# Issuing every second streamed weight piece from GpSimd's queue

## The chip, the cores and the metric

The kernel runs on one core of one Trainium2 chip. The metric is the device time of one execution in microseconds (us); lower is better. The engines are named as in the profile: PE (TensorE) with its weight loads PEld, DVE (VectorE), ACT (ScalarE), POOL (GpSimd) and SP (SyncE). A transfer (DMA) is issued by an instruction on the queue of SP or of POOL, and carried by 16 DMA engines that the queues share. In the profile, q1 (hardware_dynamic) holds the transfers that SP issued, q0 (software_dynamic) those of POOL.

## The reference: what is computed

Two independent attention layers on 2048 tokens of width 640, whose outputs stand side by side. Part A is a sliding, dilated local attention with 32 heads of 20. Part B, in which the change lies, is a recurrence over 64 segments of 32 tokens with 8 memory rows:

```
mem = mem0
for s in range(n_seg):                      # 64 segments
    h = concatenate([mem, x[32 s : 32 s + 32]])          # 40 x 640
    q, k, v = h @ Wq, h @ Wk, h @ Wv                     # 32 heads of 192: 6144 columns each
    p = softmax(mask(q k^T * scale))
    o = (p @ v) @ Wo                                     # 40 x 640
    mem = o[:8]; out[s] = o[8:]
```

The memory rows that a segment leaves are the input of the next one, so the segments follow each other. All of Wq, Wk, Wv and Wo is needed in each of them.

## The kernel before

Part A comes first, and during it part B's data are prepared: windows of x are gathered in DRAM, transposed and stored again (L353 to L380), part B's resident weights are loaded, and the weight pieces that don't fit on the chip are copied into DRAM tiles of their own, row by row as they will be wanted (`copy_streamed`, L297 to L308; tiles wcopy_k, wcopy_v, wcopy_o).

Part B cuts the weights into pieces ("units"). A k, q or v piece is 128 rows by 1536 columns (384 KB), an o piece 128 by 1280 (320 KB). `STREAMED` (L259, L260) lists those that are not resident. In each segment 24 are streamed: 11 of k, 2 of v, 11 of o; no q piece is. After the last segment, `project_late` (L656) goes through the o pieces four more times, so 11 o pieces are streamed four times more.

`get_unit` (L421 to L435) hands a piece to PE. A resident one is returned; a streamed one is loaded into a tile of the pool `wstream` (L404), which has `nbuf` = 6 slots, so that a load can begin when PE has read out the piece that stood in its slot. All of these loads are issued by SP, at L434. The users are `project32` (L475, matmuls at L483: 4 or, where 64 tokens are projected, 8 matmuls for each piece), `project_out` (L613, matmuls at L621) and `project_late` (L656, matmuls at L665).

A segment (L678 to L747) is written out by hand: projections of the four head groups, transposes, scores (L555), softmax (L560 to L572), probabilities (L580, transposed at L587), the mix with the values (L604), output projections (L621), and the memory rows for the next segment (L635). The order on PE and SP is the written one: the whole loop stands in

```python
with tc.manual_schedule(engines={mybir.EngineType.PE, mybir.EngineType.SP}):
    for s in range(n_seg):
        segment(s)
```

POOL, DVE and ACT are not in that set; the framework's planner orders their instructions when the program is built.

What POOL does in part B: it copies "late" tokens (the last 8 columns of a window, projected once in four segments and kept in tiles Lb) into QT and KT before the scores that read them (L528); it copies the same columns of the mixed output OT into OL (L611, 4 a segment); it clears a part of P (L578); and it issues three stores a segment, OL to DRAM (L728, 96 KB) and the two halves of the segment's output (L746, 15 KB each). In the last segment it also loads the stored OL back in pieces of 1.5 MB (`load_late`, L653, L654) for `project_late`. SP's other work in part B is one load of the segment's tokens HX (L467, 80 KB) and, in the first segment, resident pieces (L339).

`evacuate` (L461) copies PSUM to SBUF on ACT and DVE in turn; its line in the profile is L463.

Of the kernel before, what the change touches and what calls it, by code (L numbers as in the profile page):

```python
# [273 lines left out]
def part_b(ctx, tc, B_x, B_mem0, B_Wq, B_Wk, B_Wv, B_Wo, out, ident, n_seg, pre, nbuf, mid):  # L274
    nc = tc.nc
# [16 lines left out]
    def unit_cols(u):  # L292
        return 1280 if u[0] == "o" else 1536

    copied = {}
# [41 lines left out]
    def load_resident(units, engs):  # L337
        for k, u in enumerate(units):
            engs[k % len(engs)].dma_start(unit_tile(res[u], u), unit_src(u))  # L339
# [77 lines left out]
    wait.update(resident[n_pre + len(early):])  # L417

    ahead_of = []

    def get_unit(u):  # L421
        if u in res:
            if u in wait:
                wait.remove(u)
                load_resident([u], [nc.sync])
            return res[u]
        if wait:
            ahead_of.append(u)
            if len(ahead_of) > nbuf:
                v = next(v for v in resident if v in wait)  # L430
                wait.remove(v)
                load_resident([v], [nc.sync])
        t = wstream.tile([128, SLOT], BF16, tag="ws")
        nc.sync.dma_start(t[:, 0:unit_cols(u)], copied[u])  # L434
        return t[:, 0:unit_cols(u)]  # L435

    mask = cpool.tile([128, L], FP32)
# [37 lines left out]
    def project32(Xs, m, g, dcs=range(5), ps=None):  # L475

        if ps is None:
            ps = [ps_acc.tile([128, 384], FP32, tag="acc", name=f"acc{n}") for n in range(len(Xs))]
        for dc in dcs:
            w = get_unit((m, g, dc))  # L480
            for n, X in enumerate(Xs):
                for j in range(4):
                    nc.tensor.matmul(ps[n][32 * j:32 * j + 32, :], lhsT=X[:, dc, :],  # L483
                                     rhs=w[:, 384 * j:384 * j + 384],
                                     start=(dc == 0), stop=(dc == 4), tile_position=(0, 32 * j))
        return ps
# [126 lines left out]
    def project_out(Y, g, pairs=range(6)):  # L613
        for a in pairs:
            i = 6 * g + a
            w = get_unit(("o", i, 0))
            for r in range(2):
                c = 2 * a + r
                for gv in range(2):
                    n, at = 640 * r + 320 * gv, 64 * r + 32 * gv  # L620
                    nc.tensor.matmul(Y[at:at + 32, :], lhsT=OT[:, L * c:L * c + 32], rhs=w[:, n:n + 320],  # L621
                                     start=(i == 0), stop=(i == 23), tile_position=(0, at))
# [33 lines left out]
    def project_late(b):  # L656
        X = late_tokens(b).rearrange("p (t c) -> p t c", c=48)
        ps = [ps_acc.tile([128, 384], FP32, tag="acc", name=f"late{gv}") for gv in range(2)]
        for i in range(24):
            w = get_unit(("o", i, 0))  # L660
            for r in range(2):
                c = 2 * i + r
                for gv in range(2):
                    n = 640 * r + 320 * gv
                    nc.tensor.matmul(ps[gv][:, 0:320], lhsT=X[:, :, c], rhs=w[:, n:n + 320],  # L665
                                     start=(c == 0), stop=(c == 47))
        rows = out2.rearrange("(s n) d -> s n d", n=SEG)[LATE * b:LATE * b + LATE, SEG - M:SEG]
        for gv in range(2):
            if gv:
                y = one.tile([128, 384], BF16, tag="Vst", name="y")[:, 0:320]  # L670
            else:
                y = one.tile([128, 4, L], FP32, tag="t1", name="y")[:].rearrange("p a n -> p (a n)").bitcast(BF16)
            evacuate(y, ps[gv][:, 0:320])
            nc.gpsimd.dma_start(rows[:, :, Dm + 320 * gv:Dm + 320 * gv + 320], y)
# [83 lines left out]
def run_all(ctx, tc, A_x, A_wqkv, A_wo, B_x, B_mem0, B_Wq, B_Wk, B_Wv, B_Wo, out, ident):  # L758
    n_seg = B_x.shape[1] // 32

    def mid(emit_loads):
        with ExitStack() as actx:
            part_a(actx, tc, A_x, A_wqkv, A_wo, out, ident, emit_loads)

    part_b(ctx, tc, B_x, B_mem0, B_Wq, B_Wk, B_Wv, B_Wo, out, ident, n_seg=n_seg, pre=110000, nbuf=6,
           mid=mid)
# [59 lines left out]
```

## Time and profile before

| | us |
|---|---|
| three runs, median | 2056.71 |
| three runs, lowest and highest | 2046.49 to 2058.95 |
| the profiled execution | 2051.98 |
| its span, first to last instruction | 2050.0 |
| PE busy | 1856.2 |
| DVE busy | 1189.1 |
| ACT busy | 731.4 |
| POOL busy | 425.8 |

The page's first part has the busy time of each engine. Instructions that only issue a DMA are not counted as busy, so POOL's share does not hold its DMA issues. The third part splits the DMA traffic by queue: packets, MB, and the time its packets took as a share of what 16 engines have in the span. The chain is followed back from the last instruction to what released each step; its shares say where the span went. A group of instructions is shown as its line, engine and operation, with its busy time and the mean of one in ns, and, after the second bar, the idle time of the engine just before and what ended most of it. The DMA issues have the size of one and the median time from issue to landing.

### The profile page before, as it was taken

The numbers are of one execution on the slowest core, as the hardware profiler recorded it, in microseconds if no ns is written. First come the engines' busy times: TensorE is split into PE (matmuls) and PEld (weight loads), VectorE is DVE, ScalarE is ACT, GpSimd is POOL, SyncE is SP. The second block draws the span as 40 slices with busy tenths as digits, with TensorE's granted clock in tenths as the row PEclk, the third lists the DMA queues.
The fourth block names the chain that finished last, engine by engine and source line by source line (L and its number), as shares of the span: only waits on it lengthen the run. The fifth ranks groups of instructions, "written<-read, shape, count | busy, mean of one in ns | idle before, by whom it ended". The sixth has DMA issues, their size and how long they took to land.

```text
span 2050.0 us, 99035 instructions
## 1 busy us (share of the span) xinstructions
PE 1856.2 (91%) x42896; PEld 1136.2 (55%) x42896; DVE 1189.1 (58%) x3754; ACT 731.4 (36%) x2194; POOL 425.8 (21%) x1018
## 2 busy tenths in 40 slices
PE   7889999999899999999999898999999999999978
PEld 4555555555555555555555555555555555555557
DVE  5666565665566555566555566565556656665630
ACT  3454333333333333333333333333333333333310
POOL 2111212222221222221222221122222222222210
PEclk9999999999999999999999999999999999999989
DMA  8997999999999999999999999999999999999997
GB/s 252 311 321 260 338 332 317 337 329 325 318 324 323 313 341 322 308 329 324 321 335 323 319 320 313 328 331 330 327 327 325 335 320 340 331 328 324 327 321 232
DMA packets 302367, 654.89 MB, mean 319 GB/s; under 512 B 64297, under 2 KB 87401, under 8 KB 301929
## 3 DMA queue, kind: packets, MB, share of 16 engines
q1 hardware_dynamic: 289961, 624.64, 89.4%
q0 software_dynamic: 11968, 23.91, 3.3%
q8 instruction: 336, 5.51, 1.0%
q14 instruction: 102, 0.84, 0.1%
HBM read 623.77 MB, written 30.74 MB: 319 GB/s over the span
## 4 chain that ended last, share of the span: by engine, by line
PE 53%; DMA 30%; DVE 8%; issue 6%; SPq 2%; ACT 2%; POOL 0%; ACTq 0%; DVEq 0%; POOLq 0%
PE acc L483 25%; DMA t<-wcopy_k 19%; PE Y L621 8%; DMA t<-wcopy_o 8%; PE pt L496 5%; PE Sps L555 4%; PE OTps L604 3%; PE pq L95 3%; PE pt L587 2%; DMA t<-wcopy_v 2%; PE po L161 1%; SPq L378 1%; DVE sb L463 1%; DVE P L580 1%; PE py L172 1%
## 5 line engine op out<-in xcount | busy, mean ns | idle before, releaser
L483 PEld LDWEIGHTS <-HX 128*32 128x32 bf16 x19380 | 480.7, 97 | 345.3 <-issue 116.2
L483 PE MATMUL acc<-t,HX 128*32 128x384 bf16 x4200 | 293.4, 330 | 49.9 <-DMA t<-wcopy_k 44.4
L483 PE MATMUL acc<-wres_q,HX 128*32 128x384 bf16 x6460 | 330.9, 332 | 2.6 <-issue 2.1
L483 PE MATMUL acc<-wres_v,HX 128*32 128x384 bf16 x5812 | 320.6, 330 | 13.9 <-issue 13.8
L611 POOL COPY OL<-OT 128x96 bf16<-128x96 bf16 x256 | 172.6, 674 | 652.0 <-DVE OT L463 326.7
L463 DVE CAST sb<-acc 128x384 bf16<-128x384 f32 x308 | 170.9, 555 | 212.5 <-PE acc L483 184.6
L463 ACT CAST sb<-acc 128x384 bf16<-128x384 f32 x338 | 159.8, 473 | 320.4 <-PE acc L483 225.7
L621 PE MATMUL Y<-t,OT 128*32 128x320 bf16 x2816 | 195.1, 307 | 26.9 <-DMA t<-wcopy_o 21.6
L568 ACT ACTIVATE t<-t 128x160 f32<-128x160 f32 x256 | 86.2, 337 | 369.4 <-DVE t L567 368.6
L483 PE MATMUL acc<-wres_k,HX 128*32 128x384 bf16 x2908 | 211.1, 330 | 1.5 <-issue 1.0
L621 PE MATMUL Y<-wres_o,OT 128*32 128x320 bf16 x3328 | 207.6, 305 | 4.4 <-issue 4.4
L621 PEld LDWEIGHTS <-OT 128*32 128x32 bf16 x6144 | 136.1, 96 | 114.0 <-issue 42.3
L528 POOL COPY QT<-Lb 128x96 bf16<-128x96 bf16 x237 | 63.5, 268 | 604.0 <-PE Sps L555 552.5
L496 PE MATMUL pt<-ident,sb 128*128 128x128 bf16 x1938 | 173.0, 222 | 8.7 <-DVE sb L463 7.1
L463 DVE CAST OT<-OTps 128x120 bf16<-128x120 f32 x512 | 128.5, 275 | 67.0 <-PE OTps L604 62.6
L562 DVE SCALAR_TENSOR_TENSOR t<-Sps,mask 128x160 f32<-128x160 f32 x256 | 82.7, 323 | 133.0 <-PE Sps L555 127.2
L496 PEld LDWEIGHTS <-sb 128*128 128x128 bf16 x1938 | 110.4, 98 | 83.7 <-issue 29.6
L555 PEld LDWEIGHTS <-QT 128*64 128x64 bf16 (+1 forms) x4096 | 107.7, 109 | 86.1 <-issue 65.9
L463 ACT CAST OT<-OTps 128x120 bf16<-128x120 f32 x512 | 111.2, 259 | 107.1 <-PE OTps L604 98.1
L555 PE MATMUL Sps<-KT,QT 128*64 128x40 bf16 (+1 forms) x4096 | 141.5, 190 | 2.3 <-issue 2.2
L463 ACT CAST QT<-pt 128x384 bf16<-128x384 f32 (+1 forms) x177 | 84.9, 480 | 115.9 <-PE pt L496 115.9
L570 DVE TENSOR_REDUCE sm<-t 128x4 f32<-128x160 f32 x256 | 81.7, 319 | 76.5 <-ACT t L568 76.2
(89 smaller groups left out, 2283.7 us busy)
## 6 DMA issues: line engine op xcount, KB each, us to landing
t<-wcopy_k SPq DMA_DIRECT2D x704, 384.0 KB, 5.4
t<-wcopy_o SPq DMA_DIRECT2D x748, 320.0 KB, 4.9
t<-wcopy_v SPq DMA_DIRECT2D x128, 384.0 KB, 5.4
wres_q<-in_B_Wq_dram SPq DMA_DIRECT2D x20, 384.0 KB, 7.9
wres_v<-in_B_Wv_dram SPq DMA_DIRECT2D x18, 384.0 KB, 7.2
olate<-OL POOLq DMA_DIRECT2D x64, 96.0 KB, 5.7
ximages<-wres_v POOLq DMA_DIRECT2D x16, 320.0 KB, 6.1
HX<-ximages SPq DMA_DIRECT2D x64, 80.0 KB, 4.4
```

Source lines behind the costliest of these rows:

```text
L95: nc.tensor.matmul(pq[32 * d:32 * d + 32], lhsT=wcol[:, k, t, 4 * c + d, :], rhs=xTs[s][:, k, :], start=(k == 0), stop=(k == 4), tile_posi ...
L463: (nc.scalar.copy if copies["n"] % 2 else nc.vector.tensor_copy)(dst, src)
L483: nc.tensor.matmul(ps[n][32 * j:32 * j + 32, :], lhsT=X[:, dc, :], rhs=w[:, 384 * j:384 * j + 384], start=(dc == 0), stop=(dc == 4), tile_ ...
L496: nc.tensor.matmul(pt[:, c], lhsT=sb[:, 128 * c:128 * c + 128], rhs=ident, start=True, stop=True)
L528: nc.gpsimd.tensor_copy(tokens(T)[:, :, 32:L], b[:])
L555: nc.tensor.matmul(Sps[64 * g2:64 * g2 + 64, a, :], lhsT=QT[lo:hi, L * cc:L * cc + 64], rhs=KTt[lo:hi, cc, :], start=(g2 not in seen), sto ...
L562: nc.vector.scalar_tensor_tensor(out=t1[:], in0=Sps[:], scalar=scale, in1=mask[:].unsqueeze(1).to_broadcast([128, 4, L]), op0=ALU.mult, op ...
L568: nc.scalar.activation(t1[:], t1[:], ACTF.Exp)
L570: nc.vector.tensor_reduce(out=sm[:], in_=t1[:], axis=AX.X, op=ALU.add)
L604: nc.tensor.matmul(dst, lhsT=V[32 * a:32 * a + 32, e0:e1], rhs=PT[32 * a:32 * a + 32, late, half, :], start=(wide and late == 0 and half = ...
L611: nc.gpsimd.tensor_copy(OL[:, :, 12 * g:12 * g + 12].rearrange("p n c -> p c n"), tokens(OT)[:, :, 32:L])
L621: nc.tensor.matmul(Y[at:at + 32, :], lhsT=OT[:, L * c:L * c + 32], rhs=w[:, n:n + 320], start=(i == 0), stop=(i == 23), tile_position=(0, at))
```

## The change

A counter is kept of the streamed loads. The first, third, fifth and so on are issued by SP as before; the second, fourth and so on by POOL (`nc.gpsimd`). The tiles, the slots, the pieces, their sources and the order in which PE uses them stay. SP's order stays the written one, with every second load gone; the loads on POOL are placed among POOL's other instructions by the planner.

```diff
@@ -417,6 +417,7 @@
     wait.update(resident[n_pre + len(early):])
 
     ahead_of = []
+    streamed = [0]
 
     def get_unit(u):
         if u in res:
@@ -431,7 +432,8 @@
                 wait.remove(v)
                 load_resident([v], [nc.sync])
         t = wstream.tile([128, SLOT], BF16, tag="ws")
-        nc.sync.dma_start(t[:, 0:unit_cols(u)], copied[u])
+        streamed[0] += 1
+        (nc.sync if streamed[0] % 2 else nc.gpsimd).dma_start(t[:, 0:unit_cols(u)], copied[u])
         return t[:, 0:unit_cols(u)]
 
     mask = cpool.tile([128, L], FP32)
```

## The prediction, made before the changed kernel was run

> **What bounds the kernel now.** I read the page from the top (busy shares, slices, chain), then the stretch that the change touches, then the waits of SP's queue, then the one stretch where POOL's queue carries much traffic.
>
> ```profile
> PE 1856.2 (91%) x42896; PEld 1136.2 (55%) x42896; DVE 1189.1 (58%) x3754; ACT 731.4 (36%) x2194; POOL 425.8 (21%) x1018
> ...
> q1 hardware_dynamic: 289961, 624.64, 89.4%
> q0 software_dynamic: 11968, 23.91, 3.3%
> ...
> PE 53%; DMA 30%; DVE 8%; issue 6%; SPq 2%; ACT 2%; POOL 0%; ACTq 0%; DVEq 0%; POOLq 0%
> ...
> L483 PE MATMUL acc<-t,HX 128*32 128x384 bf16 x4200 | 293.4, 330 | 49.9 <-DMA t<-wcopy_k 44.4
> L621 PE MATMUL Y<-t,OT 128*32 128x320 bf16 x2816 | 195.1, 307 | 26.9 <-DMA t<-wcopy_o 21.6
> t<-wcopy_k SPq DMA_DIRECT2D x704, 384.0 KB, 5.4
> t<-wcopy_o SPq DMA_DIRECT2D x748, 320.0 KB, 4.9
> t<-wcopy_v SPq DMA_DIRECT2D x128, 384.0 KB, 5.4
> olate<-OL POOLq DMA_DIRECT2D x64, 96.0 KB, 5.7
> HX<-ximages SPq DMA_DIRECT2D x64, 80.0 KB, 4.4
> ```
>
> The reader is to see two resources that are nearly full together: PE is busy 91% of the span and SP's queue alone takes 89.4% of the DMA engines' time. The chain alternates between them, PE 53% and DMA 30%; SP's queue has 2% and POOL none. PE's named waits for streamed pieces are 44.4 + 21.6 = 66 us. The steady stretch, and the end of the last segment beside it, from the busy times by stretch:
>
> ```profile
> 300.00:1900.00 1600.00, 1470.73 (x36450) 883.39 (x36451) 956.19 (x3259) 579.77 (x1820) 347.01 (x851) 0.99 0.94 325
> 1955.00:1975.00 20.00, 11.03 (x169) 5.25 (x169) 4.82 (x19) 2.97 (x8) 2.10 (x5) 0.70 1.03 358
> ```
>
> Columns: length, busy us of PE, weight loads, DVE, ACT, POOL, granted clock, DMA share, GB/s. In the steady 1600 us PE is busy 92%, at a granted clock of 0.99, and the DMA engines 94% at 325 GB/s. What SP's queue waits for:
>
> ```profile
> SPq L434 <- PE acc L483: 614.9, 561, 3.3
> SPq L434 <- PE Y L621: 458.1, 385, 3.7
> ```
>
> SP sits at L434 until PE frees one of the six slots, 1.1 us at a time (1073.0 / 946). The queue is never late by itself; it is held by slots. Last, the DMA view of 1955 to 1975 us, in which L654 reads 1.5 MB pieces through POOL's queue beside SP's stream:
>
> ```profile
> q0 software_dynamic: 921, 3.88, 56.7%
> q1 hardware_dynamic: 1309, 3.24, 45.6%
> ...
> t<-wcopy_o SPq DMA_DIRECT2D x5, 320.0 KB, 11.6
> ...
> t<-wcopy_k SPq DMA_DIRECT2D x2, 384.0 KB, 15.6
> ```
>
> Both queues are served at once; POOL's gets 54% of the bytes, and SP's pieces land after 11.6 and 15.6 us in place of 4.9 and 5.4.
>
> **The change, part by part.** A segment streams 24 pieces (11 k, 2 v, 11 o) and the tail 4 x 11, so 1580 in all, which the DMA issues confirm (704 + 748 + 128). 790 of them move to POOL, 12 a segment. The sum stands against the profiled execution's own 2052.0 us (span 2050.0), which is 4.7 us under the median of the runs.
>
> *Off SP's queue.* 790 issues at 0.32 to 0.36 us (the minimum and the median of L434's issues for k and o) and as many semaphore instructions of 17 ns: about 280 us. They lie beside the slot waits above, so I take 0. The end on the good side is half of the chain's 1% for L434, 10 us. Without the cover of the slot waits it would have been the 280.
>
> *Onto POOL's queue.* POOL's nearest rows are its store of 128 rows (L728, 0.55 us an issue) and of 24 rows (L746, 0.51). 790 x 0.55 = 435 us, plus 13 us of semaphores. By segment: 12 x 0.55 = 6.6 us beside 6.1 us of copies (POOL's busy time from 1000 to 1028 us), 13 of 28 us; POOL's idle time hides them. The cover that counts is the slack of the late-token copies (L528, 426 of them, 0.27 us), which PE needs for the next scores. In the timeline one ends at 1014.09 and the scores start at 1016.01; the next ends at 1017.19 and the scores start at 1021.17. One issue ahead of a copy costs 0.55 of a slack of 1.9 to 4.0 us: 0. If a quarter of the 237 QT copies had no slack it would be 59 x 0.55 = 32 us, the upper end.
>
> *The wait that comes with them.* Each POOL issue now waits for a slot, in POOL's own order; behind it stand the copies of L528, the copy of OT (L611, 0.64 to 0.78 us), the memset of P, and the stores of L728 and L746. PE's scores wait for L528, the evacuations of the next mix for L611. PE and SP keep the written order, POOL does not, so a planner places these issues and the trace of before cannot show where. Slots and late tokens are both freed by PE in PE's order, so an issue put ahead of a copy should mostly be free before it. The nearest row is SP's slot wait: 1.1 us mean, inside the slack; the longest is 3.7, 1.8 over a slack of 1.9. Ends: 0, and once a segment 64 x 1.8 = 115 us. I take 5, nearer to the mean. At the start, POOL also has part A's stores (L176, to 188.6 us) ahead of the first pieces, which SP issues from 152 us; PE needs them from 188.5. Two to three issues late: at most 6 us, within the same 5.
>
> *The transfers.* The bytes are the same. DMA time per MB from the page: q0 0.033 x 2050 x 16 / 23.91 = 45.3 us, q1 46.9. Half the streamed bytes are 286 MB, so 286 x -1.6 / 16 = -29 us if the engines bound throughout. From the window of 20 us: q0 46.8, q1 45.0, so +32 us. The ends are of opposite sign; the window's row is a load through POOL, but of short rows under heavy load, so I stay near the middle: -5. Landing through POOL (5.7 us for 96 KB, a store) beside SP's 4.4 for 80 KB gives at most 1.3 us more, which the landing of five pieces in line (5.4 us against 1.1 us a piece) covers.
>
> *The order of arrival.* Now one queue brings pieces in the order of need. With two, a piece on SP's and the next on POOL's share the engines, so the needed one lands later and its successor earlier. Upper end: each of PE's 107 named waits (74 + 33) grows by a whole piece, 0.36 MB / 325 GB/s = 1.1 us: 118 us. Lower end: half of those waits go because the successor is already there: -33. In a steady pair the later and the earlier arrival cancel, and SP's three slots still hold work for the engines; I take +8, nearer to zero.
>
> The sum: 0 + 0 + 5 - 5 + 8 = +8, so 2060 on the profile's scale and 2065 on the runs' median.
>
> The Trainium skill (DMA: Bandwidth & Descriptors, section "Issuing engines are not separate DMA queues") says that DMAs from all issuing engines share the same 16 DMA engines, so that spreading them saves only issue time. By it alone the sum would be 2057; the 358 GB/s of the window with both queues agrees only if 325 is a matter of demand, not of the queue. The same page ("Queues, rings and completion order") says that each DMA engine takes turns between queues packet by packet; the 56.7% to 45.6% of the window is in keeping with it. It is the mechanism of the first rival.
>
> **The rivals.** *Shared engines make the needed piece late (slower).* Place: PE's waits on the pieces that stay on SP. For it: landings of 11.6 and 15.6 us in the window, PE busy only 11.03 of 20 us there. Against it: POOL then had transfers of 1.5 MB; now it holds about three of 0.36. Price: the 107 waits grow by half a piece, 0.55 us, = 59 us: 2116. It decides once PE's waits on pieces exceed 66 by more than 20 us.
>
> *POOL's order holds PE (slower).* A slot wait stands ahead of a late-token copy. For it: POOL already waits 619.6 us at L528 for PE, so what is queued there is released late. Against it: the slack. Price: one wait of 1.8 us in half of the segments, 58 us: 2115.
>
> *Two queues fill the engines better (faster).* For it: 358 GB/s at share 1.03 against 325 at 0.94, and 45.3 against 46.9 us per MB. Against it: PE is 92% busy, and the window had far more in flight than six slots allow. Price: two thirds of PE's 66 us go: 2057 - 44 = 2013.
>
> That the change does nothing at all (transfers hidden anyway) is the forecast without its 8 us.
>
> **How the numbers follow.** Within 1% of 2056.7 (2036 to 2077, about what this kernel's runs can tell apart): the forecast, 0.35, own range 2040 to 2077. Late pieces 0.27 and POOL's order 0.12, both above 2077: slower 0.39. Fuller engines 0.26, below 2036. The range runs from 2005, just beyond the faster rival, to 2130, beyond both slower ones by 15 us; some 0.2 is left out, mostly where both slower ones come together.
>
> **What would show it.** POOL's issues: 790 more at L434, near 0.55 us. Right forecast: PE's waits on wcopy pieces between 55 and 90 us, DMA share 0.93 to 0.95, L528 copies not the releaser of PE's scores. First rival: landings of SP's pieces clearly longer than POOL's, PE's waits above 90. Second: PE or PEld at L555 waiting for POOL. Third: over 332 GB/s from 300 to 1900 us. I am wrong if POOL's issue of a loaded piece takes far over 0.55 us, or if the planner lets one queue take most of the slots.

## The result and the profile after

The changed kernel takes 2109.48 us (median of 4 runs, 2107.29 to 2115.85) against 2051.6 beside it: a ratio of 1.0287, 95% interval 1.0237 to 1.0336, so 58 us slower. The profiled execution has a span of 2108.2 us at a clock of 0.979 (before: 2050.0 at 0.981). Two lines were added ahead of the load, one of them right before it, so that L434, L483, L528, L555, L611 and L621 of before are now L436, L485, L530, L557, L613 and L623.

The page of the changed kernel: busy times, queues, chain, the groups of the streamed pieces, and the DMA issues.

```profile
PE 1854.8 (88%) x42896; PEld 1136.5 (54%) x42896; DVE 1191.6 (57%) x3754; ACT 734.6 (35%) x2194; POOL 828.4 (39%) x1808
...
q1 hardware_dynamic: 176201, 336.36, 49.4%
q0 software_dynamic: 75168, 312.19, 41.2%
...
DMA 43%; PE 37%; DVE 8%; issue 6%; ACT 2%; SPq 2%; POOL 1%; POOLq 0%; ACTq 0%; DVEq 0%
...
L436 POOL DMA_DIRECT2D t<-wcopy_k x384 | 207.0, 540 | 444.4 <-PE acc L485 351.7
L485 PE MATMUL acc<-t,HX 128*32 128x384 bf16 x4200 | 286.2, 329 | 79.3 <-DMA t<-wcopy_k 46.1
...
L623 PE MATMUL Y<-t,OT 128*32 128x320 bf16 x2816 | 191.3, 309 | 67.3 <-DMA t<-wcopy_o 64.2
...
L557 PE MATMUL Sps<-KT,QT 128*64 128x40 bf16 (+1 forms) x4096 | 141.0, 190 | 1.2 <-POOL QT L530 0.9
...
t<-wcopy_k POOLq DMA_DIRECT2D x384, 384.0 KB, 5.2
t<-wcopy_o SPq DMA_DIRECT2D x406, 320.0 KB, 5.1
t<-wcopy_k SPq DMA_DIRECT2D x320, 384.0 KB, 4.9
t<-wcopy_o POOLq DMA_DIRECT2D x342, 320.0 KB, 5.6
t<-wcopy_v SPq DMA_DIRECT2D x64, 384.0 KB, 5.4
t<-wcopy_v POOLq DMA_DIRECT2D x64, 384.0 KB, 6.3
```

PE does the same work (1854.8 us against 1856.2) in a longer span. The chain's DMA share grew from 30% to 43%, at PE's expense (53% to 37%). The idle time ahead of the streamed matmuls went from 49.9 and 26.9 us to 79.3 and 67.3. POOL's busy time went from 425.8 to 828.4 us, chiefly by its 790 issues at 0.54 us: unlike SP's, the issues of POOL are counted as busy on the page, and those of its stores were so before as well. (The section on the profile before says otherwise.) The scores wait 0.9 us in all, once, for POOL's late tokens: POOL's copies hold next to nobody. The view of L436 says who waited for its loads:

```profile
who waited for it (us, times):
  PE acc L485: 76.9, 107
  PE Y L623: 64.2, 72
```

The same two rows of L434 in the kernel before:

```profile
  PE acc L483: 46.4, 79
  PE Y L621: 21.6, 33
```

PE's waits for pieces doubled, by 73 us. The steady stretch of the changed kernel:

```profile
300.00:1900.00 1600.00, 1433.62 (x35631) 862.75 (x35620) 936.48 (x3186) 569.24 (x1776) 682.16 (x1505) 0.99 0.93 317
```

The DMA engines moved 317 GB/s at a share of 0.93 (before: 325 at 0.94), so they were not overrun; they were given work later. Which pieces come late shows when each load is paired, in the trace, with the end of PE's last matmul on the piece six places before it, in e6 five (whose slot it takes), with its landing, and with PE's first matmul on it. Means over all pieces that PE used from 300 to 1900 us, in us, with the runs of the next section; the last column is the ratio less 1, times 2051.6:

| kernel | slot free to issue | issue to landing | slot free to landing | landing to use | slower by |
|---|---|---|---|---|---|
| before | 0.20 | 5.18 | 5.38 | 1.20 | |
| changed, SP's pieces | 0.05 | 5.18 | 5.22 | 1.53 | |
| changed, POOL's pieces | 0.46 | 5.45 | 5.91 | 0.83 | |
| changed, all | 0.25 | 5.31 | 5.57 | 1.18 | 59 |
| all on POOL (e1) | 1.01 | 5.13 | 6.14 | 0.95 | 122 |
| every second on ACT (e2) | 0.09 | 5.51 | 5.60 | 1.03 | 26 |
| early pieces on POOL (e3) | 0.32 | 5.29 | 5.60 | 1.11 | 48 |
| late pieces on POOL (e4) | 0.33 | 5.25 | 5.58 | 1.30 | 90 |
| five slots (e6) | 0.15 | 4.79 | 4.95 | 0.93 | 145 |
| HX on POOL (e8) | 0.17 | 5.14 | 5.31 | 1.22 | -5 |
| SP alone, held back (e9) | 0.76 | 5.15 | 5.91 | 0.95 | 81 |
| both queues late (e10) | 0.49 | 5.38 | 5.87 | 0.97 | 89 |
| all on ACT (e11) | 2.99 | 4.41 | 7.40 | 0.78 | 419 |

It is POOL's pieces that come late: 41% of them were used within 0.25 us of their landing, against 9% of SP's and 19% before. Over the whole span, PE's idle time just ahead of such pieces went from 42 us (70 times) to 125 us (151 times) for the pieces that the change gives to POOL, and from 29 us (45 times) to 25 us (31 times) for those that stay on SP. The mean from landing to use hardly moved (1.20 to 1.18 us), because SP's pieces came earlier while POOL's came later: the mean lead does not show the loss, the late pieces do.

POOL issues 0.41 us later after a slot is free than SP does, and its pieces land 0.27 us later after the issue. Against the kernel before, POOL's pieces land 0.53 us later after their slot is free: about half of that is the later issue, and half (0.27) the longer way from issue to landing. A few lines of POOL's timeline in the changed kernel, with start, duration, instruction, and in brackets the idle time before it and what ended it:

```profile
1003.22 0.55 POOL L436 DMA_DIRECT2D t<-wcopy_v  x1 [1.23 <-PE acc L485]
1006.78 0.55 POOL L436 DMA_DIRECT2D t<-wcopy_k  x1 [3.01 <-PE acc L485]
1007.32 0.54 POOL L436 DMA_DIRECT2D t<-wcopy_o  x1
1007.85 0.28 POOL L530 COPY QT<-Lb 128x96 bf16<-128x96 bf16 x1
...
1026.28 0.64 POOL L613 COPY OL<-OT 128x96 bf16<-128x96 bf16 x1 [1.19 <-DVE OT L465]
1026.79 0.54 POOL L436 DMA_DIRECT2D t<-wcopy_k  x1
1027.32 0.55 POOL L730 DMA_DIRECT2D olate<-OL  x1
1027.86 0.54 POOL L436 DMA_DIRECT2D t<-wcopy_k  x1
1028.51 1.02 POOL L748 DMA_DIRECT2D out_dram<-Ysb  x2
```

Two things are to be seen. Mostly POOL stands idle at a piece until PE frees the slot (1.23 us, 3.01 us), and a piece that has nothing ahead of it is still issued 0.32 to 0.38 us after the slot is free (means over a piece's 56 or 57 segments, for eight of POOL's twelve pieces). At the end of a segment the pieces queue up behind the copy of L613 and the stores: k0_3, k1_0 and k1_3 are issued 0.66, 0.78 and 0.85 us after their slot is free. Of POOL's mean of 0.46 us, then, some 0.35 is there without anything ahead, and some 0.11 is POOL's other work.

### The profile page after: what moved, and what is told of

The parts are those of the page before. It is cut to its first block, busy times and chain, and to the rows that moved or that the text cites. A ratio compares the mean times of both kernels' runs of the same rounds, so it can differ in the third digit from the quotient of the medians.

```text
span 2108.2 us, 98914 instructions
## 1 busy us (share of the span) xinstructions
PE 1854.8 (88%) x42896; PEld 1136.5 (54%) x42896; DVE 1191.6 (57%) x3754; ACT 734.6 (35%) x2194; POOL 828.4 (39%) x1808
## 3 DMA queue, kind: packets, MB, share of 16 engines
q8 instruction: 336, 5.51, 1.0%
## 4 chain that ended last, share of the span: by engine, by line
DMA 43%; PE 37%; DVE 8%; issue 6%; ACT 2%; SPq 2%; POOL 1%; POOLq 0%; ACTq 0%; DVEq 0%
DMA t<-wcopy_o 17%; DMA t<-wcopy_k 16%; PE acc L485 15%; DMA t<-wcopy_v 9%; PE Y L623 6%; PE Sps L557 3%; PE pq L95 2%; PE OTps L606 2%; PE pt L498 2%; PE late L667 2%; PE pt L589 1%; PE po L161 1%; SPq L378 1%; DVE t L564 1%; DVE OT L465 1%
## 5 line engine op out<-in xcount | busy, mean ns | idle before, releaser
L485 PEld LDWEIGHTS <-HX 128*32 128x32 bf16 x19380 | 483.3, 96 | 360.1 <-issue 126.7
L436 POOL DMA_DIRECT2D t<-wcopy_k x384 | 207.0, 540 | 444.4 <-PE acc L485 351.7
L485 PE MATMUL acc<-t,HX 128*32 128x384 bf16 x4200 | 286.2, 329 | 79.3 <-DMA t<-wcopy_k 46.1
L485 PE MATMUL acc<-wres_q,HX 128*32 128x384 bf16 x6460 | 323.6, 328 | 1.3 <-issue 0.8
L485 PE MATMUL acc<-wres_v,HX 128*32 128x384 bf16 x5812 | 320.4, 332 | 2.6 <-issue 2.4
L436 POOL DMA_DIRECT2D t<-wcopy_o x342 | 183.9, 538 | 286.3 <-PE Y L623 133.6
L613 POOL COPY OL<-OT 128x96 bf16<-128x96 bf16 x256 | 172.7, 675 | 255.9 <-DVE sm L573 110.9
L623 PE MATMUL Y<-t,OT 128*32 128x320 bf16 x2816 | 191.3, 309 | 67.3 <-DMA t<-wcopy_o 64.2
L623 PEld LDWEIGHTS <-OT 128*32 128x32 bf16 x6144 | 136.6, 96 | 155.3 <-issue 85.8
L623 PE MATMUL Y<-wres_o,OT 128*32 128x320 bf16 x3328 | 208.3, 305 | 1.9 <-issue 1.9
L485 PE MATMUL acc<-wres_k,HX 128*32 128x384 bf16 x2908 | 208.9, 329 | 0.5 <-ACT sb L465 0.3
L557 PEld LDWEIGHTS <-QT 128*64 128x64 bf16 (+1 forms) x4096 | 107.0, 109 | 84.9 <-issue 65.5
L557 PE MATMUL Sps<-KT,QT 128*64 128x40 bf16 (+1 forms) x4096 | 141.0, 190 | 1.2 <-POOL QT L530 0.9
```

The costliest lines, as they stand in the source:

```text
L436: (nc.sync if streamed[0] % 2 else nc.gpsimd).dma_start(t[:, 0:unit_cols(u)], copied[u])
L557: nc.tensor.matmul(Sps[64 * g2:64 * g2 + 64, a, :], lhsT=QT[lo:hi, L * cc:L * cc + 64], rhs=KTt[lo:hi, cc, :], start=(g2 not in seen), sto ...
L613: nc.gpsimd.tensor_copy(OL[:, :, 12 * g:12 * g + 12].rearrange("p n c -> p c n"), tokens(OT)[:, :, 32:L])
```

## The experiments

Three theories stood at the start. A: a piece from POOL starts and lands later, and PE waits. B: two queues share the DMA engines, which changes the order of arrival. C: POOL's other work stands ahead of the pieces. All kernels below compute the whole result; the ratios are against the kernel before on the same chip.

**All pieces on POOL (e1).**

```diff
-        (nc.sync if streamed[0] % 2 else nc.gpsimd).dma_start(t[:, 0:unit_cols(u)], copied[u])
+        nc.gpsimd.dma_start(t[:, 0:unit_cols(u)], copied[u])
```

> All 1580 streamed pieces are issued by POOL, so there is one queue for them again, in the order of need. Theory A (a piece from POOL starts about 0.6 us later after its slot is free, and pieces with less slack than that make PE wait): all pieces are late instead of half, so about twice the 58 us of the change, 2165 us (2130 to 2200). Theory B (two queues share the DMA engines, and the arrival out of order is the cost): back near the kernel before, 2052 us, at most 2075. Theory C (the other work in POOL's order stands ahead of the pieces): twice the cost again, and POOL's issues late mainly behind the copies of OT and the stores.

Measured: 2171.66 us, ratio 1.0596 (1.0537 to 1.0656). With one queue again B expects no loss; the loss doubled, as A and C expected. A piece lands 5.13 us after its issue, as with SP alone (5.18), so a load through POOL was not slower on its way when all went there; it is issued 1.01 us after its slot is free. The steady stretch of this kernel:

```profile
300.00:1900.00 1600.00, 1404.17 (x33960) 833.50 (x33952) 893.94 (x3031) 538.73 (x1692) 979.31 (x2082) 0.98 0.89 303
```

The DMA share falls to 0.89: engines idle for want of issued pieces. Part of the 1.01 us is C, POOL's own work, and part the issues of the pieces ahead, 0.54 us each; this run does not tell them apart.

**Which pieces go through POOL (e3, e4).** In place of the counter, a set of 12 pieces says which go to POOL, chosen by how long ahead of its use a piece landed in the kernel before. In e3 the early ones go to POOL, in e4 the others. The edit of e3, against the kernel before:

```diff
+    on_pool = {("k", 0, 1), ("k", 0, 3), ("k", 1, 0), ("v", 0, 0), ("k", 2, 1), ("k", 2, 4), ("o", 0, 0), ("o", 2, 0), ("k", 3, 1), ("o", 6, 0), ("o", 12, 0), ("o", 18, 0)}
...
-        nc.sync.dma_start(t[:, 0:unit_cols(u)], copied[u])
+        (nc.gpsimd if u in on_pool else nc.sync).dma_start(t[:, 0:unit_cols(u)], copied[u])
```

> 12 pieces a segment go through POOL as in the change, but those that landed 1.25 us or more ahead of their use in the kernel before (k0_1, k0_3, k1_0, v0_0, k2_1, k2_4, o0, o2, k3_1, o6, o12, o18). Theory A: they can lose 0.6 us without making PE wait, so 2052 to 2070 us. Theory B: the same bytes share the engines in two queues, so like the change, 2105 to 2115. Theory C: POOL has the same amount of work, so about like the change too.

> The other 12 pieces of a segment go through POOL: those that landed 0.3 to 1.0 us ahead of their use in the kernel before. Theory A: nearly each of them makes PE wait, so clearly slower than the change, 2130 to 2180 us. Theory B and theory C: like the change, 2105 to 2115, since the number of pieces and the bytes on each queue are about the same.

Measured: e3 2098.82 us, ratio 1.0233 (1.0193 to 1.0273); e4 2141.54 us, ratio 1.0437 (1.0385 to 1.0489). The number of pieces and nearly the bytes are those of the change, so by B or C alone all three would take the same time. e4 does not; it came out as A expected, which bears out A's point that the slack of the late piece counts. e3 and the change cannot be told apart by their intervals, and e3 is a miss for A in its simple form: with 1.25 us or more of slack, pieces should have borne it. They did not, since a slack is not a property of a piece: k0_1, k0_3 and k1_0 follow each other on POOL, and k1_0's landing came 0.21 us ahead of its use, after 1.92 in the kernel before: it was issued 0.71 us later after its slot was free, and it was 1.45 us longer on its way.

**SP alone, in two transfers (e5, and later e12).** Every second piece is issued as 16 and 112 rows, and in e12 as 64 and 64. Against the changed kernel:

```diff
-        (nc.sync if streamed[0] % 2 else nc.gpsimd).dma_start(t[:, 0:unit_cols(u)], copied[u])
+        n, lo = unit_cols(u), 0
+        if streamed[0] % 2 == 0:
+            nc.sync.dma_start(t[0:16, 0:n], copied[u][0:16])
+            lo = 16
+        nc.sync.dma_start(t[lo:128, 0:n], copied[u][lo:128])
```

> All pieces stay on SP; every second one is issued as two transfers, 16 rows first and then 112, so that 7/8 of it starts one SP issue (0.32 to 0.4 us) later. One queue, POOL as before. Theory A: a later start alone costs, 0.38/0.6 of 58 us = 37 us, so 2089 us (2070 to 2105). Theories B and C: no second queue and no work on POOL, so 2052 us within 15.

> All pieces on SP, every second one issued as two transfers of 64 rows each, so that half of it starts one SP issue (0.35 us) later. It asks why the run with 16 and 112 rows took 2538 us. If a second transfer for a piece were itself the cost: slow again, 2400 us or more. If the cut at row 16 was (an engine's share of the rows no longer the same as in a whole piece): DMA time per MB back at 47 us, and by theory A only the later half counts, 2052 to 2080 us.

Measured: 2537.84 us, ratio 1.2359 (1.2311 to 1.2406), and for the halves 2605.78 us, ratio 1.2696 (1.2622 to 1.277). e5 misses every expectation; e12 is the first of its two cases, slow again. They say nothing on the three theories, because the transfers themselves got slower. The queue's line of e12, with the share of the engines' span:

```profile
q1 hardware_dynamic: 302601, 624.69, 96.7%
```

The 624.6 MB that took 89.4% of 2050.0 us before, now 624.69, take 96.7% of 2602.2: 64.4 us of engine time per MB (x 16 / 624.69) in place of 46.9. It is not the uneven cut, since the even one is no better. From 300 to 1900 us the packets of 3072 bytes have a median of 195 ns, before 121. The whole pieces slowed too: 54% of the k and v pieces are cut in two, but 80% of these packets took 166 ns or more. Why is left open.

**SP alone, every second piece held back (e9).** A clean form of what e5 was to ask: the load gets a dependency on a later matmul of PE.

```diff
...
-        nc.sync.dma_start(t[:, 0:unit_cols(u)], copied[u])
+        load = nc.sync.dma_start(t[:, 0:unit_cols(u)], copied[u])
+        now[0] = n = len(last_of)
+        if n % 2 == 1 and n >= 6:
+            after = done[min(last_of[n - 6] + 12, len(done) - 1)]
+            tc.add_manual_dep(load.ins, after.name, ...)
```

`done` lists the matmuls in order, `last_of` has the last one on each streamed piece; the lines that fill them are left out here.

> One queue, all pieces on SP and POOL as in the kernel before; every second piece is held back, after its slot is free, until PE is 12 matmuls (about 0.5 us of work) further. Theory A (the late start of every second piece is the cost): 2100 us (2085 to 2130), with the held pieces as those that PE waits for. Theory B (two queues share the DMA engines and change the order of arrival): 2052 us within 15.

Measured: 2128.84 us, ratio 1.0395 (1.0348 to 1.0441). One queue, POOL untouched, and the loss is there: late starts alone cost it. The delay came out larger than meant (held pieces 0.96 us after their slot is free, and 0.57 for the others, which stand behind them in SP's order), in the mean 0.53 us later to landing than before. The price is 81 / 0.53 = 153 us per us of mean lateness; e1 gives 122 / 0.76 = 161.

**Every second piece on ACT's queue (e2), and all of them (e11).**

```diff
-        (nc.sync if streamed[0] % 2 else nc.gpsimd).dma_start(t[:, 0:unit_cols(u)], copied[u])
+        (nc.sync if streamed[0] % 2 else nc.scalar).dma_start(t[:, 0:unit_cols(u)], copied[u])
```

> Every second piece goes through ACT's queue, a second queue that is not POOL's. Theory B: two queues share the engines as in the change, so 2110 us or more, with longer times from issue to landing on one of the queues. Theory A: if ACT's issues start as soon as the slot is free, 2052 to 2075 us; ACT's evacuations behind a slot wait could cost more, and then ACT's copies, not the landing of pieces, are what PE waits for.

> All pieces on ACT's queue: one queue for them again, with ACT's order. It tells what the 26 us of the run with every second piece on ACT were. If two queues sharing the engines were the cost (theory B): back to 2050 to 2062 us, landing after 5.2 us. If slot waits in ACT's order were the cost: about twice, 2100 us or more, with PE waiting for ACT.

Measured: e2 2074.98 us, ratio 1.0128 (1.007 to 1.0186), far under B's 2110; e11 2467.27 us, ratio 1.2043 (1.1961 to 1.2124). In e2 both queues issue at once (0.05 and 0.14 us), and pieces still land later on both: 5.53 and 5.50 us after the issue, against 5.18. Its issues:

```profile
t<-wcopy_k ACTq DMA_DIRECT2D x384, 384.0 KB, 5.6
t<-wcopy_o SPq DMA_DIRECT2D x406, 320.0 KB, 5.5
t<-wcopy_k SPq DMA_DIRECT2D x320, 384.0 KB, 5.5
t<-wcopy_o ACTq DMA_DIRECT2D x342, 320.0 KB, 5.2
```

So here a second queue, with next to no delay of the issue, comes with a way some 0.3 us longer, evenly on both, and e2's 26 us fit it (0.22 us in all at 153 us is 34). That is B, as a part of the loss: in the change the way grew by 0.14 us in the mean (5.18 to 5.31), all of it on POOL's pieces, and in e1, with one queue, it did not. e11 was to tell whether the 26 us were ACT's order; it can't, because with all pieces there they are issued 2.99 us after their slot is free, in the mean. How much of e2's 26 us is ACT's waiting stays open.

**Five slots (e6).** In the kernel before, `nbuf=6` becomes `nbuf=5`.

> The kernel before with five slots for streamed pieces instead of six, so each piece is issued one piece (1.15 us) later. It shows what lead is worth. Theory A: the change takes 0.3 us of lead from the mean piece for 58 us, so a whole piece of lead costs 150 to 250 us, 2200 to 2300. If it costs under 60 us, a late start of 0.6 us on every second piece can't be what costs 58.

Measured: 2194.22 us, ratio 1.0709 (1.0661 to 1.0757), 145 us, just under the range. PE's wait for k pieces:

```profile
PE acc L483 <- DMA t<-wcopy_k: 155.0, 196, 3.8
```

It was 44.4 us before. A slot is 1.15 us of lead (1385 pieces were used in the 1600 us before), so 145 / 1.15 = 126 us per us: of the size that e9 and e1 give. The kernel has no slot's lead to spare.

**HX on POOL (e8).** In the kernel before, only the load of L467 becomes `nc.gpsimd.dma_start`.

> The kernel before with only the load of the segment's tokens (HX, 64 transfers of 80 KB, used a segment later) moved from SP to POOL, so that SP can issue the pieces behind it at once. Theory A: lead is what counts, and the pieces o0 and o2 that stand behind this load gain 0.4 to 0.6 us each, so a little faster, 2040 us (2025 to 2052). Theory B: some traffic moves to the second queue; 2052 to 2065.

Measured: 2041.7 us, ratio 0.9976 (0.9942 to 1.001). The mean piece is issued 0.03 us sooner and lands 0.07 sooner; 0.07 x 153 is 11 us, and the interval of -12 to +2 us holds both that and nothing. It is no proven gain.

**The change once more, and with SP's pieces late too (e10).** e10 is the changed kernel with e9's dependency, 7 matmuls on, on the loads that stay on SP.

```diff
...
+        if streamed[0] % 2 and n >= 6:
+            after = done[min(last_of[n - 6] + 7, len(done) - 1)]
+            tc.add_manual_dep(load.ins, after.name, ...)
```

> The changed kernel once more, beside the two kernels below on the same chip: 2105 to 2115 us by each theory.

> The change, with SP's pieces held back as well, after their slot is free, until PE is 7 matmuls (some 0.4 us) further, so that both queues start a piece about equally late. Theory A as a mean (what counts is how late the mean piece lands): 0.2 us more on the mean piece, at the price of the run with held pieces on SP alone (80 us for 0.53 us), so 30 us slower than the change, 2140 us. Theory A as unevenness (SP's pieces that land early only hold slots and wait for POOL's): little to lose, 2095 to 2120 us.

Measured: the change again 2115.64 us, ratio 1.0305 (1.0238 to 1.0372); e10 2137.17 us, ratio 1.0434 (1.0366 to 1.0501). The theory that only the unevenness between the queues counts falls: evening them out by delay (0.51 us on SP, 0.47 on POOL) cost some 26 us more (1.0434 against 1.0305). The number is the one expected of the mean, in part by luck: the mean piece came 0.30 us later, not 0.2, which at 153 us would have been 46. Every kernel of the table whose mean piece lands later after its slot is free is slower. The mean does not give the change's size by itself, though.

## Why the prediction was right and wrong

The range of 2005 to 2130 held the 2109; the likeliest single case, no change, was wrong, and the first rival ("the needed piece late", 2116 us) had the kind of wait right: PE's waits on pieces rose by 73 us, past the 20 us that I set for it. That its price of 59 us met the measured 58 is luck. It let each of 107 waits grow by 0.55 us; instead the waits in the two rows became more, 112 to 179, and grew by 0.18 us in the mean (0.61 to 0.79). And it had the wrong piece. I argued from the window in which POOL's queue held 1.5 MB transfers that SP's pieces would be the late ones; with pieces of 0.36 MB SP's landed as before (5.18 us) and POOL's late (5.45). Two of the signs set for the forecast came true without it: the DMA share of 0.93, and scores that do not wait for POOL.

Step by step:

- *Off SP's queue*, 0: right, and a little better than nothing; SP's pieces are issued 0.05 us after their slot is free (before 0.20). Its good end misread the chain, which gives SP at L434 5.6 us, 0.3%; the 1% is that of L378.
- *Onto POOL's queue*, 0.55 us an issue, hidden: right. 0.54 measured, POOL 39% busy, the late tokens hold the scores for 0.9 us. The 6.1 us taken as copies already held 1.6 us of the stores' issues.
- *The wait that comes with them*, 5: right about those behind (the second rival, POOL's order holding PE, falls by the same 0.9 us). Not seen was the reverse: POOL's own work, and the 0.3 us that POOL takes to start an issue, hold the piece back. The trace of before had that row, the store of L728 issued 0.30 us after the copy that it waited for (in all, times, longest):

```profile
POOL olate L728 <- POOL OL L611: 18.7, 63, 0.3
```

- *The transfers*, -5: engine time per MB of both queues together is (0.494 + 0.412) x 2108.2 x 16 / 648.55 = 47.1 us, against 46.9 on SP's queue before. About nothing, as taken.
- The step that failed stands there too: "at most 1.3 us more, which the landing of five pieces in line ... covers". The line in flight does not cover it, because the next load is issued only when a slot comes free: what is added between a free slot and the landing is taken from the lead. PE was named as waiting 107 times before, so for those pieces the lead was already used up; that row should have priced every added 0.1 us. What was added, for POOL's pieces: 0.53 us.
- *The order of arrival*, +8: the mis-sized term, by about 50 us. Counted in the trace, PE's idle time just ahead of pieces that had landed less than 0.25 us before grew by 79 us, all of it on POOL's pieces (42 to 125; SP's 29 to 25), and 20 us of it came back in PE's other idle time: PE stood idle 188 us in all before and 247 after. What sets the 79 is less clear. Slot free to landing grew by 0.19 us in the mean; at the 153 us of e9 that is 29 us. The other 30 are put down to unevenness: SP's pieces land 0.16 us earlier, which only holds slots, and POOL's 0.53 later. That split is argued, not shown. For it speak that SP's pieces held PE no more than before, and that even runs cost 118 to 182 us per us (e2, e9, e1, e10) and uneven ones 218 (e3), 310 (the change) and 450 (e4); against it, that e3 and e4 differ so much with the same lateness, so which pieces are late enters as well.
- *Two queues fill the engines better*: no, 317 GB/s.

The Trainium skill (DMA: Bandwidth & Descriptors, section "Latency and other measured facts") gives some 0.6 us to the first byte for SP's path and some 1 us for GpSimd's. That difference of 0.4 us is near the 0.41 us by which POOL's issue comes later than SP's here, but no run here shows a first byte, and e1's landing times show no such difference after the issue.

## What to carry to other kernels

Where a stream of loads lives on a few slots, ask what stands between a free slot and the next landing, and price each tenth of a us of it by the stream's waits; busy shares and bandwidth hardly showed it here, nor did the mean lead. The second queue added no bandwidth to engines that were 94% busy (317 GB/s against 325), and POOL's queue, on an engine with work of its own, started a load 0.46 us after its slot was free, where SP's took 0.05. Before moving loads, take away a slot: if that costs (here 145 us), expect lateness to cost too.

## What the runs showed of the hardware

A stream in which every second piece goes in two parts of 64 rows is far dearer as a whole than one of whole pieces of 128 rows: 64.4 us of engine time per MB against 46.9 (e12), and 63.4 with parts of 16 and 112 (e5). The Trainium skill (DMA: Bandwidth & Descriptors, section "Rules for kernel authors") advises one transfer of 128 rows over two of half the rows, since the two share the same engines; the runs agree that it does not pay; the price is 0.24 (e5) and 0.27 (e12) of this kernel's time.

Where PE waited much, its own work took longer too: its 42896 matmuls took 1856.2 us at a mean granted clock of 0.981 before, 1898.4 at 0.974 with five slots, and 1993.4 at 0.936 with all pieces on ACT, so in these two runs the loss is more than the waits. In the changed kernel it is not so (1854.8 us at 0.979), and no run here shows what lowers the clock.
